# Phi first on the SP hardware queue, and tokens 1536-2559 in one store

## Chip, cores, metric

One core of one Trainium2 chip. The metric is device microseconds of one execution; lower is better. A time is the median over several runs of a kernel. The profiled execution of a kernel is one of these runs. A span is counted from its first instruction, and is some 1.8 us shorter than the time.

## The reference

Sliding-window attention on 8 batches of 8 heads (576 tokens, head size 64), and then a soft mixture of experts on its output, with 4608 tokens of width 512, 32 slots and 8 experts:

```python
x = attn(q, k, v).transpose(0, 2, 1, 3).reshape(4608, 512)   # window 32; half of the heads with dilation 4
logits = x @ phi                                             # phi: 512 x 32
d = softmax over tokens (logits);  slot_input = d.T @ x
for e in range(8):
    h = relu(slot_input[e] @ w1[e]);  slot_out[e] = h @ w2[e]   # w1: 512 x 1024, w2: 1024 x 512, f32
c = softmax over slots (logits);   out = c @ slot_out        # 4608 x 512, f32
```

## The kernel before

A list scheduler written in Python simulates all engines at build time and fixes the order of the instructions on each. Q, K, V and nearly all weights come over GpSimd's software queue, which casts f32 to bf16, in an order that is chained by hand. Two loads go over SP's hardware queue: the first half of expert 0's w1 (1 MB, uncast, converted by ScalarE) at the very start, and phi (64 KB), which waits for the first transpose on VectorE. SP also issues all output stores.

```python
    op(SP, lambda: spq.dma_start(                       # "the first w1 piece"
        af(w2off(0), [[1, 2048]]),
        w1_rows(0)[:, :2048]), .1, -200.0,              # last number: priority, low goes first
       kind="dma", nbytes=1 << 20, sem=sem("s_w1f"), writes=b_w2[0], name="w1f")
    for x in range(2):
        op(ACT, ...)                                    # f32 -> bf16 of that piece
    ...
    def load_phi(first):
        op(SP, lambda: spq.dma_start(
            f(o_phst, [[64, 2], [1, 64]]),
            moe_phi.rearrange("(hf p two) s -> p hf (two s)", hf=2, two=2)), .1, 20.0,
           kind="dma", nbytes=65536, sem=sem("s_phi"), writes=[b_phst], name="phi", after=[first])
        for g in range(2):
            op(DVE, lambda g=g: dve.tensor_copy(...), .2, -20.0,     # "the casts of phi"
               reads=[b_phst], writes=[b_phis])
    ...
    GROUPS = [(0, 4), (512, 4), (1024, 4), (1536, 8), (2560, 8), (3584, 8)]   # first token, 128-token tiles
    ...
    for G, js in [(2, (2, 3))] + [(G, range(8)) for G in range(3, 6)]:        # the last output tiles
        for j in js:
            out_tile(G, j, 0, 512, T2 + 10 + G + .1 * j)                      # matmul, eviction by ACT or DVE
            if j == js[-1] or G == 3 and j == 3:
                n = 4 if G == 3 else len(js)                                  # group 3 leaves in two stores
                store(G, 0, 512, T2 + 10 + G + .1 * j + .05, j + 1 - n, n)
```

The softmax here doesn't subtract the row's maximum and nothing guards it: scores larger than these inputs give would overflow.

Of the kernel before, what the change touches and what calls it, by code (L numbers as in the profile page):

```python
# [58 lines left out]
class Sched:  # L59
# [8 lines left out]
    def op(self, eng, fn, dur, prio, reads=(), writes=(), rmw=(), after=(), banks=(), name="",  # L68
           kind="c", nbytes=0, rate=422e3, lag=0.0, sem=None, tail=False):
        o = Op()  # L70
        o.eng, o.fn, o.dur, o.prio, o.name = eng, fn, dur, prio, name
        o.kind, o.bytes, o.rate, o.lag, o.sem, o.tail = kind, nbytes, rate, lag, sem, tail
        o.deps, o.succ = set(), []
        o.banks, o.opens, o.ord = [], [], None
        o.seq = len(self.ops)
        for a in after:
            if a is not None:
                o.deps.add(a)
        for b in reads:
            o.deps.update(b.w)  # L80
            b.r.append(o)
        for b in writes:
            if b.r:
                b.prev = b.w + b.r
                b.w, b.r = [], []
            o.deps.update(b.prev)
            b.w.append(o)
        for b in rmw:
            o.deps.update(b.prev)
            o.deps.update(b.w)  # L90
            o.deps.update(b.r)
            b.w.append(o)
        for b in list(reads) + list(writes) + list(rmw) + list(banks):
            if isinstance(b, Bank) and b not in o.banks:
                o.banks.append(b)
                if b.left == 0:
                    o.opens.append(b)
                b.left += 1
        o.deps.discard(o)
        self.ops.append(o)  # L100
        return o
# [99 lines left out]
def bass_dilated_sliding_attn__then__soft_moe_slots_kernel(  # L201
# [56 lines left out]
    o_phst, o_sid, o_rv, o_rinv, o_csp, o_rcol = 0, 128, 640, 704, 744, 760  # L258
# [3 lines left out]
    def a(off, dims, p0=0, pn=128):  # L262
        return AP(ar, p0 * NBF + off, [[NBF, pn]] + dims)
# [4 lines left out]
    def af(off, dims, p0=0, pn=128):  # L268
        return AP(ar_f.tensor, (p0 * NBF + off) // 2, [[NBF // 2, pn]] + dims)

    def f(off, dims, p0=0, pn=128):
        return AP(fs, p0 * FSW + off, [[FSW, pn]] + dims)
# [9 lines left out]
    op = sc.op  # L282
    PE, ACT, DVE, POOL, SP = "PE", "ACT", "DVE", "POOL", "SP"
    pe, act, dve, pool, spq = nc.tensor, nc.scalar, nc.vector, nc.gpsimd, nc.sync
# [7 lines left out]
    def dvet(n, psum=False):  # L292
        return ((120 if psum else 58) + n) / 960.0

    b_id, b_mp, b_md, b_oh, b_sel, b_rm, b_phst, b_phis = (Buf(n) for n in
        ("id", "mp", "md", "oh", "sel", "rm", "phst", "phis"))
# [21 lines left out]
    def w2off(e):  # L318
        return o_w2 + e * 8 * DM if e < 5 else o_stg + (e - 5) * 8 * DM


    def sem(n):
        return [nc.alloc_semaphore(n), 0]
# [13 lines left out]
    def load_batch(b):  # L337
        s = b % NSTG
        for j, x in LOADS[b > 0]:
            def fn(j=j, x=x, src=(q, k, v)[j][b, 4 * x:4 * x + 4]):  # L340
                o = o_stg + (s * 3 + j) * 2304
                if j == 0 or b == 0:
                    return pool.dma_start(a(o + 1152 * x, [[1, 1152]]),  # L343
                                          src.rearrange("h (p t) d -> (h p) (t d)", p=32))
                return pool.dma_start(AP(ar, x * NBF + o, [[2 * NBF, 64], [1, 2304]]),  # L345
                                      src.rearrange("h (u t) d -> (h u) (t d)", u=16))
            dma_in(fn, 128 * 1152 * 4, s_stg[s][j][x], (-100.0 if b < 1 else -80.0) + 2 * b,
                   f"ld{b}{'qkv'[j]}{x}", writes=[b_stg[s][j][x]] if j == 0 or b == 0 else b_stg[s][j])
# [14 lines left out]
    def w1_rows(e):  # L363
        return moe_w1[e].rearrange("(p four) f -> p (four f)", four=4)
# [28 lines left out]
    def load_w(n):  # L393
# [12 lines left out]


    op(SP, lambda: spq.dma_start(
        af(w2off(0), [[1, 2048]]),
        w1_rows(0)[:, :2048]), .1, -200.0,  # L410
       kind="dma", nbytes=1 << 20, sem=sem("s_w1f"), writes=b_w2[0], name="w1f")
# [59 lines left out]
        bb.prev, bb.w = bb.prev + bb.w, []  # L471
    first_t = []

    def load_phi(first):
        op(SP, lambda: spq.dma_start(
            f(o_phst, [[64, 2], [1, 64]]),
            moe_phi.rearrange("(hf p two) s -> p hf (two s)", hf=2, two=2)), .1, 20.0,
           kind="dma", nbytes=65536, sem=sem("s_phi"), writes=[b_phst], name="phi", after=[first])
        for g in range(2):
            op(DVE, lambda g=g: dve.tensor_copy(  # L480
                a(o_phis + 4 * g, [[128, 4], [32, 4], [1, 4]]),
                f(o_phst + 16 * g, [[32, 4], [4, 4], [1, 4]])), .2, -20.0,
               reads=[b_phst], writes=[b_phis])
# [293 lines left out]
    def row_sums(g0, n, prio):  # L777
        t0, nj = GROUPS[g0]
        w = 32 * nj * n
        bank = Bank(f"rs{g0}")  # L780

        def fn():
            last = None
            for qd in range(4):
                last = pe.matmul(pf(bank.idx, 0, [[1, w]], 32 * qd, 32), a(o_rm, [[1, 32]]),
                                 a(o_et + t0 + 32 * nj * qd, [[128 * nj, n], [1, nj], [nj, 32]]),
                                 start=True, stop=True)
            return last

        op(PE, fn, pet(4, w), prio, reads=[b_et, b_rm], writes=[bank], name=f"RS{g0}")  # L790
        op(DVE, lambda: dve.transpose(af(o_rt, [[1, w]]), pf(bank.idx, 0, [[1, w]])),
           .1 + w / 960, prio + .1, reads=[bank], writes=[b_rt], name=f"RT{g0}")
        op(DVE, lambda: dve.reciprocal(f(rcol(g0), [[1, w // 32]]), af(o_rt, [[32, w // 32]])),
           .2, prio + .2, reads=[b_rt], writes=[b_rinv], name=f"RR{g0}")

    last_ex = [None]
    for i in range(NH):
        if i % 2 == 0:
            load_batch(i // 2)
        half(i)  # L800
        if i == 0:
            load_phi(first_t[0])
        if i in RS_AT:
            for g, n in RS_AT[i]:
                row_sums(g, n, RSP * PERIOD + 16)
# [7 lines left out]
    for x, y in zip(dma_order, dma_order[1:]):  # L813
# [7 lines left out]
       writes=[b_rcol], name="cs")  # L821
# [17 lines left out]
    for x in range(2):  # L839
# [12 lines left out]
        for g in range(2):  # L852
# [5 lines left out]
            writes=[b_hsb[x], b_p[0], b_p[1]], name=f"RL{x}")  # L858
# [20 lines left out]
    def l2(es, x, col, n, cs=range(8), bufs=None):  # L879
# [22 lines left out]
       name="SOx")  # L902
# [19 lines left out]
    def ostg(G):  # L922
        return o_w1 + 8 * GROUPS[G][0]
# [25 lines left out]
    def store(G, c0, cw, prio, j0, n):  # L949
        t0, nj = GROUPS[G]  # L950
        rd = [b_og[G][j][s] for j in range(j0, j0 + n) for s in range(2)
              if c0 < 256 * (s + 1) and c0 + cw > 256 * s]
        dst = out[t0:t0 + 128 * nj, c0:c0 + cw].rearrange("(p j) f -> p j f", j=nj)[:, j0:j0 + n, :]
        src = af(ostg(G) + 2 * (512 * j0 + c0), [[512, n], [1, cw]])
        store_ops.append(op(SP, lambda: spq.dma_start(dst, src), .1, prio, kind="dma",
                            nbytes=128 * n * cw * 4, rate=347e3 if cw < 512 else 420e3,
                            sem=sem(f"s_o{G}{c0}{j0}"), reads=rd, name=f"ST{G}{c0}{j0}"))

    T2 = T1 + 40
# [9 lines left out]
    for G, js in [(2, (2, 3))] + [(G, range(8)) for G in range(3, 6)]:  # L969
        for j in js:  # L970
            out_tile(G, j, 0, 512, T2 + 10 + G + .1 * j)
            if j == js[-1] or G == 3 and j == 3:
                n = 4 if G == 3 else len(js)
                store(G, 0, 512, T2 + 10 + G + .1 * j + .05, j + 1 - n, n)

    order = sc.run([4, 5, 6, 7], [0, 1, 2, 3], last_ex[0])

# [8 lines left out]
    for o in order:  # L986
# [5 lines left out]
        for d in o.deps:  # L992
            if d.eng == o.eng == PE:
                continue
            s, val = d.ev
# [60 lines left out]
```

## Time and profile before

| | before |
|---|---|
| time, median of 3 | 177.01 us (176.88 to 177.13) |
| span of the profiled run | 175.2 us |
| bytes moved in it, as the page counts HBM traffic | 61.93 MB read, 9.44 MB written |
| last packet of the last weight slab ends | 151.23 us |
| last store packet ends | 174.41 us |

The last two are from the trace's records of single DMA packets. The main views stand in the prediction below. Two more are needed. The first is the timeline of SP and of ScalarE at the start, with start, length, what, and in brackets the idle time before it and what ended that:

```profile
0.74 0.37 SPq L408 DMA_DIRECT2D ar<-in_moe_w_dram  x1
11.85 0.38 SPq L475 DMA_DIRECT2D fs<-in_moe_phi_dram  x1
...
5.67 2.00 ACT L413 ACTIVATE ar<-ar 128x1024 bf16<-128x1024 f32 x2 [3.65 <-DMA ar<-in_moe_w_dram]
```

The first w1 piece is the first thing SP does; it has landed when ScalarE converts it at 5.67. The second view is the DMA engines' first microseconds, by stretches (the last two columns are the busy share of the 16 DMA engines and the GB/s written):

```profile
core 0: us, PE busy (x) PEld busy (x) DVE busy (x) ACT busy (x) POOL busy (x), PEclk, DMA share, GB/s
1.00:2.00 1.00, 0.00 (x0) 0.00 (x0) 0.72 (x2) 1.00 (x1) 0.77 (x2) 1.00 0.61 106
2.00:3.00 1.00, 0.00 (x0) 0.00 (x0) 0.85 (x1) 0.02 (x1) 1.00 (x3) 1.00 0.73 180
3.00:4.00 1.00, 0.00 (x0) 0.00 (x0) 0.87 (x1) 0.00 (x0) 1.00 (x3) 1.00 0.82 344
4.00:5.00 1.00, 0.00 (x0) 0.00 (x0) 1.00 (x6) 0.00 (x0) 1.00 (x3) 1.00 1.08 434
```

Nothing moves in the first 1.7 us.

### The profile page before, as it was taken

The page shows a single profiled execution, that of the slowest core. Times are in us where ns is not written, and L with a number is a line of the kernel's source. Part 1 is how long each engine was busy: PE and PEld are TensorE (multiplying, and loading weights), DVE is VectorE, ACT ScalarE, POOL GpSimd, SP SyncE. Part 2 cuts the span into 40 slices and gives each one's busy share as a digit, 9 for nine tenths or more (in the row PEclk, how much of TensorE's full clock was granted, in tenths as well). Part 3 has the DMA queues.
Part 4 walks back from the last instruction along what each step waited for, and adds up shares of the span by engine and source line. Part 5 has one row for each costly group of instructions (what it writes and reads, how often), then busy time and mean ns, then how long its engine had stood idle before and what let it go on. Part 6 is the DMA issues. An engine that isn't in the chain of part 4 may idle for free.

```text
span 175.2 us, 4785 instructions
## 1 busy us (share of the span) xinstructions
PE 127.4 (73%) x2102; PEld 86.0 (49%) x2102; DVE 120.7 (69%) x220; ACT 105.1 (60%) x165; POOL 44.5 (25%) x90
## 2 busy tenths in 40 slices
PE   0008667969998998998988997999776766898000
PEld 0005535746766866776756766776343323442000
DVE  6899497978998998998698798349430002699300
ACT  2404763797978969969868968965603001599000
POOL 7659502406234053027200014940000000000000
PEclk9999995699999999999999999999999999999655
DMA  6999999999999999999999999999999999999997
GB/s 191 228 210 217 211 214 208 219 210 213 216 211 214 217 213 207 218 211 217 213 209 216 217 213 221 215 219 211 209 223 215 210 192 189 270 343 418 449 423 299
DMA packets 14388, 41.26 MB, mean 236 GB/s; under 512 B 1696, under 2 KB 7328, under 8 KB 12064
## 3 DMA queue, kind: packets, MB, share of 16 engines
q0 software_dynamic: 10512, 30.41, 88.3%
q1 hardware_dynamic: 3856, 10.55, 15.7%
q8 instruction: 16, 0.26, 0.5%
q14 instruction: 4, 0.03, 0.0%
HBM read 61.93 MB, written 9.44 MB: 407 GB/s over the span
## 4 chain that ended last, share of the span: by engine, by line
DMA 33%; DVE 24%; PE 22%; ACT 7%; POOL 5%; issue 3%; POOLq 0%; DVEq 0%
DMA ar<-in_moe_w_dram 21%; DMA ar<-in_v_dram 12%; PE ps L529 6%; DVE ar L497 6%; DVE ar L945 6%; ACT ar L568 4%; POOL ar L381 3%; DVE ar L503 3%; PE ps L590 2%; PE ps L713 2%; PE ps L536 2%; DVE ar L634 2%; PE ps L623 2%; PE ps L546 2%; DVE ar L454 2%
## 5 line engine op out<-in xcount | busy, mean ns | idle before, releaser
L568 ACT ACTIVATE ar<-ps 128x1152 bf16<-128x1152 f32 (+1 forms) x32 | 37.9, 1186 | 21.5 <-PE ps L553 10.9
L529 PE MATMUL ps<-ar 128*128 128x320 bf16 (+1 forms) x128 | 23.2, 306 | 16.1 <-DVE ar L503 13.8
L497 DVE STREAM_TRANSPOSE ar<-ar 128x576 uint32<-128x576 uint32 x28 | 32.8, 1237 | 0.6 <-DMA ar<-in_v_dram 0.6
L634 DVE TENSOR_TENSOR ar<-ps,fs 96x768 bf16<-96x768 f32 (+1 forms) x32 | 26.3, 822 | 1.1
L596 ACT ACTIVATE ar<-ps 128x768 bf16<-128x768 bf16 x32 | 24.8, 809 | 3.6 <-PE ps L590 3.1
L529 PEld LDWEIGHTS ps<-ar 128*128 128x128 bf16 x128 | 10.8, 100 | 20.9 <-POOL ar L427 13.7
L623 PE MATMUL ps<-ar 128*128 128x65 bf16 x320 | 15.2, 195 | 3.4 <-ACT ar L568 2.1
L590 PE MATMUL ps<-ar 128*128 128x128 bf16 x192 | 15.8, 229 | 2.4 <-DVE ar L634 2.1
L503 DVE STREAM_TRANSPOSE ar<-ar 128x576 uint32<-128x576 uint32 x12 | 14.6, 1241 | 1.8 <-DMA ar<-in_q_dram 1.8
L623 PEld LDWEIGHTS ps<-ar 128*128 128x128 bf16 x320 | 12.1, 98 | 6.7 <-ACT ar L568 2.9
L345 POOL DMA_DIRECT2D ar<-in_k_dram x14 | 7.5, 541 | 30.5 <-DVE ar L497 15.6
L942 ACT ACTIVATE ar<-ps,fs 128x512 f32<-128x512 f32 (+1 forms) x23 | 11.4, 636 | 5.7 <-PE ps L934 5.7
L590 PEld LDWEIGHTS ps<-ar 128*128 128x128 bf16 x192 | 12.7, 118 | 3.7 <-DVE ar L634 2.3
L630 DVE RECIPROCAL fs<-ps 96x12 f32<-96x12 f32 (+1 forms) x32 | 6.5, 203 | 10.9 <-PE ps L623 10.6
L885 PE MATMUL ps<-ar 128*32 128x512 bf16 (+1 forms) x76 | 10.8, 347 | 4.3 <-DMA ar<-in_moe_w_dram 3.3
L945 DVE TENSOR_SCALAR ar<-ps,fs 128x512 f32<-128x512 f32 (+1 forms) x23 | 12.7, 627 | 1.0 <-PE ps L934 1.0
L934 PE MATMUL ps<-ar 128*128 128x512 bf16 (+1 forms) x46 | 10.2, 346 | 1.1 <-DVE ar L909 1.0
L343 POOL DMA_DIRECT2D ar<-in_q_dram x16 | 8.8, 549 | 6.1 <-DVE ar L509 6.1
L713 PE MATMUL ps<-ar 128*128 128x288 bf16 x64 | 9.8, 299 | 0.7 <-ACT ar L697 0.7
L693 ACT ACTIVATE ar<-ps 128x1024 bf16<-128x1024 bf16 x8 | 8.2, 1030 | 3.3 <-PE ps L680 3.3
L690 ACT ACTIVATE ar<-ps 128x576 bf16<-128x576 bf16 x16 | 9.5, 648 | 1.1 <-PE ps L674 0.8
L509 DVE STREAM_TRANSPOSE ar<-ar 128x160 uint32<-128x160 uint32 (+1 forms) x32 | 9.6, 413 | 0.0
(78 smaller groups left out, 190.2 us busy)
## 6 DMA issues: line engine op xcount, KB each, us to landing
ar<-in_moe_w_dram POOLq DMA_DIRECT2D x13, 1024.0 KB, 26.6
ar<-in_k_dram POOLq DMA_DIRECT2D x16, 288.0 KB, 14.5
ar<-in_q_dram POOLq DMA_DIRECT2D x16, 288.0 KB, 16.2
ar<-in_v_dram POOLq DMA_DIRECT2D x16, 288.0 KB, 15.2
out_dram<-ar SPq DMA_DIRECT2D x2, 2048.0 KB, 10.1
out_dram<-ar SPq DMA_DIRECT2D x10, 256.0 KB, 3.1
out_dram<-ar SPq DMA_DIRECT2D x2, 1024.0 KB, 6.1
ar<-in_moe_w_dram SPq DMA_DIRECT2D x1, 1024.0 KB, 4.9
```

The source lines that it names most:

```text
L497: return dve.transpose(au(o_kqv[kq] + 2304 * j + 36 * x, [[1, 18], [36, 16], [576, 2]]), au(src + 64 * 18 * x, [[32, 18], [1, 32]]))
L503: return dve.transpose(au(dst, [[1, 18], [18, 32]]), au(src, [[32, 18], [1, 32]]))
L529: pe.matmul(pf(h, 0, [[1, W]]), a(o_id, [[1, 128]]), a(msk, [[1, W]]), start=True, stop=False)
L568: eo = op(ACT, lambda P=P, W=W: act.activation(a(P, [[W, 4], [1, W]]), AP(ps, 0, [[4096, 128], [512, 4], [1, W]]), ACTF.Exp, scale=SCALE), ...
L590: last = pe.transpose(pb(bank.idx, bb * 256 + par * 32, [[64, 4], [1, 32]]), src, a(o_id, [[1, 128]]))
L596: op(ACT, lambda t=t, bank=bank: act.activation(a(o_vb[vs] + 3 * t * VBK, [[66, 12], [2, 32], [1, 2]]), pb(bank.idx, 0, [[64, 12], [1, 32] ...
L623: last = pe.matmul(pf(bank.idx + x, 65 * t, [[1, 65]]), w, a(VB + t * VBK + 66 * h, [[1, 65]]), start=True, stop=True)
L634: op(DVE, lambda hp=hp, bank=bank: dve.tensor_tensor(a(ox + 128 * hp, [[64, 2], [256, NT], [1, 64]], 0, rows), pf(bank.idx, 0, [[512, 2], ...
L713: last = pe.matmul(pf(bank.idx, 0, [[1, 288]]), a(o_phis + 128 * c, [[1, 128]]), a(o_xt[xt] + 576 * c + 288 * g, [[1, 288]]), start=(c == ...
L885: last = pe.matmul(pf(sobank[x].idx, 0, [[1, n]], 32 * j, 32), a(o_htz + 1024 * g + 128 * c + 32 * j, [[1, 32]]), a(w2off(e) + DM * c + co ...
L942: op(ACT, lambda: act.activation(dst, src(), ACTF.Copy, scale=sca), actt(cw, .1), prio + .1, reads=[bank, b_rinv], writes=wr, name=f"OE{G} ...
L945: op(DVE, lambda: dve.tensor_scalar(dst, src(), sca, None, op0=AluOp.mult), dvet(cw, True) + .08, prio + .1, reads=[bank, b_rinv], writes= ...
```

## The change

The intent: phi is out of the way before anything else, and the output of tokens 1536-2559 leaves in one store with longer rows. The whole diff:

```diff
+    op(SP, lambda: spq.dma_start(
+        f(o_phst, [[64, 2], [1, 64]]),
+        moe_phi.rearrange("(hf p two) s -> p hf (two s)", hf=2, two=2)), .1, -201.0,
+       kind="dma", nbytes=65536, sem=sem("s_phi"), writes=[b_phst], name="phi")
     op(SP, lambda: spq.dma_start(
         af(w2off(0), [[1, 2048]]),
         w1_rows(0)[:, :2048]), .1, -200.0,
@@
-    def load_phi(first):
-        op(SP, lambda: spq.dma_start(
-            f(o_phst, [[64, 2], [1, 64]]),
-            moe_phi.rearrange("(hf p two) s -> p hf (two s)", hf=2, two=2)), .1, 20.0,
-           kind="dma", nbytes=65536, sem=sem("s_phi"), writes=[b_phst], name="phi", after=[first])
+    def load_phi():
         for g in range(2):
             op(DVE, lambda g=g: dve.tensor_copy(
@@
-            load_phi(first_t[0])
+            load_phi()
@@
             out_tile(G, j, 0, 512, T2 + 10 + G + .1 * j)
-            if j == js[-1] or G == 3 and j == 3:
-                n = 4 if G == 3 else len(js)
-                store(G, 0, 512, T2 + 10 + G + .1 * j + .05, j + 1 - n, n)
+        store(G, 0, 512, T2 + 10 + G + .1 * js[-1] + .05, js[0], len(js))
```

## The prediction

> **What bounds the kernel now.** I read the page first, its rows by slices, and looked for a resource that is never idle:
>
> ```profile
> PE   0008667969998998998988997999776766898000
> DVE  6899497978998998998698798349430002699300
> DMA  6999999999999999999999999999999999999997
> HBM read 61.93 MB, written 9.44 MB: 407 GB/s over the span
> ```
>
> Each digit is a fortieth of 175.2 us. PE and VectorE have holes; the DMA row is 9 in all slices but the first and last. The kernel has to move 71.4 MB, and it does so at 407 GB/s on average. It is a transfer-bound kernel, and its time is: the moment the DMA engines start, plus the work queued for them, plus their bubbles, plus the last completion.
>
> Next I checked where the chain of waits enters the DMA queue:
>
> ```profile
> 79.68 20.95 DMA ar<-in_v_dram
> ...
> 115.33 36.21 DMA ar<-in_moe_w_dram
> 151.54 0.04 issue
> ...
> 152.84 8.63 DVE ar L945 x15
> 161.47 0.66 DVEq L1026
> 162.13 1.32 DVE ar L945 x2
> ```
>
> Columns are start, length, what. A V load issued at 79.7 landed 21 us later, and the last weight slab issued at 115.3 landed 36 us later: GpSimd issues far ahead, and the loads stand in a queue. A buffer that comes free a microsecond earlier or later upstream only changes how long they stand. The chain then ends in evictions up to 163.5, but the span goes on for another 11.7 us, in which nothing but DMA works. So I read the busy time by stretches:
>
> ```profile
> core 0: us, PE busy (x) PEld busy (x) DVE busy (x) ACT busy (x) POOL busy (x), PEclk, DMA share, GB/s
> 5.00:80.00 75.00, 58.43 (x1102) 42.60 (x1104) 66.37 (x112) 53.84 (x79) 28.36 (x60) 0.95 1.07 213
> 80.00:148.00 68.00, 56.70 (x947) 37.53 (x946) 37.44 (x78) 38.58 (x64) 12.18 (x21) 1.00 1.08 212
> ...
> 149.00:150.00 1.00, 0.97 (x10) 0.63 (x7) 1.00 (x4) 1.00 (x4) 0.00 (x0) 1.00 0.77 103
> ...
> 158.00:164.00 6.00, 3.29 (x12) 0.97 (x9) 5.45 (x9) 4.17 (x8) 0.00 (x0) 0.96 1.03 421
> 164.00:174.00 10.00, 0.00 (x0) 0.00 (x0) 0.00 (x0) 0.00 (x0) 0.00 (x0) 0.50 1.02 433
> ```
>
> The DMA share is at or above 1 from 5 us to 148 us and again to 174 us; the GB/s of the load stretches count bytes written as bf16, half of the f32 bytes read. In the packet records, at a quarter microsecond, the only slots under 0.97 are the start (first packet at 1.70, shares of 0.56 to 0.88 up to 2.75), 148.75 to 150.25 (the hand-over from slabs to stores), one slot at 154.0, and the end. The change touches neither of the two middle ones.
>
> **What the Trainium skill says.** All four are sections of the page "DMA: Bandwidth & Descriptors". "Issuing engines are not separate DMA queues": transfers of all issuers run on the same 16 engines and interleave. So moving phi moves work within one budget and takes none away; the shares above agree. "SWDGE vs HWDGE vs iDMA": an engine has 16 internal queues and round-robins between them. The trace agrees: phi's 256 packets of 256 B, issued at 11.85 beside a full software queue, ran from 15.55 to about 20, mostly singly among the loads' packets. "Latency and other measured facts": first byte of a hardware-queue transfer about 600 ns. The first w1 piece was issued at 0.74 for 0.37 us and its first packet began at 1.70, so 0.6 us after the issue: agrees. "Why small descriptors are slow (HBM only)": a fixed cost of about 3 cycles per packet. The records show medians of 311 ns for an 8192 B store packet and 615 for a 16384 B one: two of the former cost 7 ns more than one of the latter, so the overhead is there and tiny.
>
> **Part one, phi first.** Its work is 256 packets, 16 per engine, at a median of 18 ns: 0.29 us on each engine. Removed: these 0.29 us from 15.6 to 20. Added: the same at about 1.7. The first w1 piece is issued 0.38 us later (the old phi issue took 0.384), so its packets begin at about 2.1 and end at about 5.6 instead of 5.25. The activations that convert it (from 5.67) start 0.35 us later; their output is used only at 129.9, and ScalarE is idle until 15.53, so nothing waits.
>
> What counts is the load queue. Its first packets begin at 4.7 whatever SP does, and would then share the engines with 0.35 us more of the w1 piece. So the stream is up to 0.35 us late from 5.6 on. It gets back phi's share near 16. I looked closely there: the half w1 load finished its packets on the engines at 15.68 to 16.24, and the next load (issued only at 12.37, after GpSimd had waited for its masks) finished at 17.27 to 17.99. It needs 4 packets of 361 ns, 1.44 us, but took 1.59 on the first engine and 1.75 on the last. On the last engine 0.31 us were lost: that is phi. On the first, 0.15 us: there phi sat in a small bubble before the next load's descriptors arrived. In the new kernel the late stream covers that bubble. Sum of the part: +0.35 at the start in the worst case, -0.31 near 16, so +0.04; if phi's small packets fit into the slow start (first w1 packets took 565 to 919 ns against 309 later), down to -0.3. I take -0.0, plus or minus 0.3.
>
> The two VectorE casts of phi (180 ns each, at 20.86) move forward: their data is there, and only the dependence on the first transpose held the load back. The list scheduler will probably put them ahead of the first key transpose at 10.57. First scores, at 13.76, are then about 0.3 us later. This has slack: loads stand in the queue, and the last PE stretch before the final weights idles anyway:
>
> ```profile
> 135.58 3.61 PE L885 MATMUL ps<-ar 128*32 128x512 bf16 x40 [0.54 <-DVE ar L870]
> 141.45 3.02 PE L885 MATMUL ps<-ar 128*32 128x512 bf16 x12 [2.26 <-DMA ar<-in_moe_w_dram]
> ```
>
> PE waited 2.26 us for weights, so all the compute before may be 2 us later free of charge.
>
> **Part two, one store for tokens 1536-2559.** Two stores of 1 MB (8 KB rows, 256 packets) become one of 2 MB (16 KB rows, 128 packets). Per engine: 16 x 311 = 4.98 us become 8 x 615 = 4.92, plus one completion packet of 9 ns less: -0.06 us, and this lies on the path, as the stores run back to back to 174.2. One issue of about 0.6 us on SP goes, beside other work: SP was waiting for evictions.
>
> The price is a later start. The first half was issued at 156.96; the single store can only be issued when the eighth tile is evicted, where the second half was issued: 158.26. With 0.92 us from issue to first packet (first output store: issued 149.25, packets from 150.17) it is ready at 159.18. The store before it, 512 KB, finished on the engines at 159.33 to 159.59. So the queue just doesn't run dry: 0.15 us to spare on the earliest engine. Cost 0, at worst 0.2.
>
> Sum: 177.01 + 0.0 - 0.06 + 0 = 176.95; I allow a trifle for the thin margin and say 176.98.
>
> **The rivals.** (1) A bubble before the merged store. For it: a margin of 0.15 us against a latency known from a few stores. Against: two measured issues (0.74 and 149.25) agree on 0.92 to 0.96. If the hardware queue needed 0.5 us more, +0.35: 177.3. (2) The late first w1 piece delays all loads and nothing is given back: +0.35, 177.35. For it: the stream has no bubbles later in which to recover. Against: the 0.31 us that phi takes today on the slowest engine. (3) Phi hides wholly in the cold start and its 0.3 us near 16 go: 176.65. For it: the engines are under-used until 2.75. Against: SP issues in order, and the w1 piece moves back by a whole issue. (4) The scheduler's greedy order changes everywhere, because estimated times shift by 0.16 us (65536 B at its 422 GB/s), and compute ends later than the weights. For it: the order of all engines comes from one simulated run. Against: order of loads is fixed by explicit chaining, loads are 20 to 36 us ahead, 2.26 us are free at the end. Were it 4 us worse, about 179; I give it 2 in 100. (5) The intended gain, fewer and larger packets, being worth more than 2%: 3.5 us; the whole overhead of small rows in this store is 0.06.
>
> **Range and chances.** The central rivals span 176.65 to 177.35, and three runs of one kernel spread by 0.25. Hence 177.0, 176.6 to 177.45. Faster by 2% would need 173.5, which the bytes forbid: 1 in 100. Slower by 2% (180.6) only by a bad reshuffle: 2 in 100.
>
> **What would show each step.** The w1 piece's issue at about 1.1 and ScalarE's first conversion near 6.0 show the delay; the casts of phi near 10.6 show the move; the last slab's landing near 151.5 tells the net of part one. Fourteen stores instead of fifteen, the merged one issued near 158.3, and a DMA share of 1 between 158 and 161 show part two; a share of 0.8 at 159 would be rival 1. I am wrong if the last slab lands more than 0.5 us off 151.5, or if PE no longer waits for weights at 141.

## The result

| | before | after |
|---|---|---|
| time, median of 6 | 177.07 us (176.88 to 177.13) | 177.44 us (177.28 to 177.78) |
| ratio of the means | | 1.0024, 95% interval 1.0012 to 1.0037 |
| span of the profiled run | 175.2 us | 176.0 us |
| first packet of the first w1 piece | 1.74 us | 2.33 us |
| last packet of the last weight slab ends | 151.23 us | 151.76 us |
| last store packet ends | 174.41 us | 175.20 us |

A ratio here and below is the mean time of one kernel's fast runs over that of the other's of the same rounds, so it is not quite the ratio of the medians. The change makes the kernel slower by about 0.4 us. That is small, but the interval excludes 1, and the prediction had said nil. The median lies at the very edge of the predicted range, which ends at 177.45. (The prediction gives 1.70 for the first w1 packet before; read to the hundredth, it is 1.74.)

The profiled run of the changed kernel was the slowest of its six, 177.78, so its 0.8 us must not be read as the effect. The same views as before, for the changed kernel. First the start:

```profile
0.74 0.42 SPq L408 DMA_DIRECT2D fs<-in_moe_phi_dram  x1
1.21 0.46 SPq L412 DMA_DIRECT2D ar<-in_moe_w_dram  x1
...
7.11 1.06 ACT L417 ACTIVATE ar<-ar 128x1024 bf16<-128x1024 f32 x1 [5.09 <-DMA ar<-in_moe_w_dram]
```

```profile
1.00:2.00 1.00, 0.00 (x0) 0.00 (x0) 0.72 (x2) 1.00 (x1) 0.77 (x2) 1.00 0.13 32
2.00:3.00 1.00, 0.00 (x0) 0.00 (x0) 0.85 (x1) 0.02 (x1) 1.00 (x3) 1.00 1.10 197
3.00:4.00 1.00, 0.00 (x0) 0.00 (x0) 0.87 (x1) 0.00 (x0) 1.00 (x3) 1.00 0.74 254
4.00:5.00 1.00, 0.00 (x0) 0.00 (x0) 1.00 (x6) 0.00 (x0) 1.00 (x3) 1.00 0.99 406
```

The w1 piece is issued 0.47 us later than before, and ScalarE can convert it 1.44 us later (7.11 against 5.67). More than the issue is behind that: by the packet records its last packet ends at 6.59 instead of 5.29, as from 4.71 on it shares the engines with the first K load. Between 3 and 4 us only 254 GB/s flow instead of 344. ScalarE itself loses nothing: it was idle until its first exponential anyway. What is lost is DMA time, and this kernel has no other.

Then the long stretches and the tail:

```profile
DMA  5999999999999999999999999999999999999997
```

```profile
153.74 8.63 DVE ar L945 x15
```

```profile
5.00:80.00 75.00, 58.06 (x1109) 42.53 (x1113) 66.22 (x113) 53.92 (x79) 28.14 (x60) 1.00 1.07 214
80.00:148.00 68.00, 56.40 (x945) 37.40 (x939) 37.33 (x77) 38.53 (x63) 12.42 (x21) 1.00 1.08 212
...
150.00:151.00 1.00, 1.00 (x6) 0.46 (x3) 1.00 (x3) 1.00 (x4) 0.00 (x0) 0.50 0.76 109
151.00:152.00 1.00, 1.00 (x10) 0.77 (x10) 0.60 (x2) 0.38 (x1) 0.00 (x0) 0.50 1.11 335
...
158.00:164.00 6.00, 4.19 (x14) 1.37 (x13) 6.00 (x10) 5.07 (x9) 0.00 (x0) 1.00 1.05 426
164.00:174.00 10.00, 0.00 (x0) 0.00 (x0) 0.35 (x1) 0.00 (x0) 0.00 (x0) 0.61 1.02 434
```

The long stretches move at the same rate: nothing in the middle is slower, the stream is only later. The last evictions begin at 153.74 instead of 152.84, 0.90 later, although the last slab's packets ended only 0.53 later. The rest goes with the column before the DMA share: the clock granted to PE was 0.50 in this run from 149.1 to 152.5, as the trace's clock records say, just where the last expert's matmuls run between the last loads and the first full stores. The Trainium skill, "TensorE: Matmul & The Clock Gate", part 1, says that an idle PE falls to half clock, and that the window in which this is judged is free-running, so that the phase differs from run to run. The traces are compatible with the second half, but only one run of each kernel was kept, so they do not test it: in the profiled run of the kernel before, the half-clock stretch before the tail lay at 26.9 to 33.8, and there again with the merged store alone, in that of phi first alone (below) at 142.9 to 146.3 and 40.5 to 43.9, in that of the dummy load there was none. None of the nine other kept traces has one between 148 and 160. What it goes with can be counted in the packet records: from 148 to 156 the DMA engines were idle for 0.76 us in this run and for 0.40 in the kernel before, and most of the difference is a gap at 154.75 to 155.25 (shares of 0.25 and 0.29), where the stores waited for evictions. So some 0.4 us of this run's lateness arose in the tail, and most likely belong to this execution and not to the change; no second profile of the kernel was kept to show that.

To follow the lateness of the stream, I took all load packets from the packet records (256-byte phi packets left out), added up the f32 bytes that they had read by a given moment, a packet in flight by its share, and divided the shortfall against the kernel before by 419 GB/s, the rate of 16 engines at one 16 KB source packet per 625 ns. "Behind" below is this, in us, to about 0.01:

| kernel | first bulk packet | at 4 us | at 15 us | at 17 us | at 30 us | at 148 us |
|---|---|---|---|---|---|---|
| after | 2.33 | 0.55 | 0.62 | 0.37 | 0.28 | 0.26 |
| phi first alone | 2.31 | 0.68 | 0.74 | 0.50 | 0.40 | 0.37 |
| phi second | 1.74 | 0.04 | 0.27 | 0.03 | -0.07 | -0.06 |
| phi on ScalarE's queue | 1.74 | 0.05 | 0.26 | 0.01 | -0.08 | -0.05 |
| dummy load first | 2.23 | 0.57 | 0.64 | 0.50 | 0.64 | 0.60 |
| phi twice | 2.62 | 1.12 | 1.43 | 1.18 | 1.09 | 1.00 |
| merged store alone | 1.76 | -0.03 | 0.05 | 0.06 | 0.04 | 0.04 |

The first row is the loss and the repayment of the changed kernel: 0.6 us behind from the start, 0.34 given back between 15 and 30, and the rest kept. The other rows are the experiments.

### The profile page after: what moved, and what is told of

Its sections match the earlier page's. It is cut to its first block, busy times and chain, and to the rows that moved or that the text cites. A ratio compares the mean times of both kernels' runs of the same rounds, so it can differ in the third digit from the quotient of the medians.

```text
span 176.0 us, 4782 instructions
## 1 busy us (share of the span) xinstructions
PE 127.3 (72%) x2101; PEld 86.4 (49%) x2102; DVE 120.8 (69%) x220; ACT 105.3 (60%) x165; POOL 44.5 (25%) x90
## 4 chain that ended last, share of the span: by engine, by line
DMA 44%; DVE 25%; PE 13%; ACT 4%; POOL 4%; issue 3%; DVEq 0%
DMA ar<-in_v_dram 24%; DMA ar<-in_moe_w_dram 20%; DVE ar L497 8%; DVE ar L945 6%; PE ps L529 3%; DVE ar L503 3%; PE ps L590 2%; ACT ar L568 2%; DVE ar L458 2%; POOL ar L381 2%; DVE ar L634 2%; PE ps L934 1%; POOL ar L345 1%; DVE ar L463 1%; PE ps L885 1%
## 5 line engine op out<-in xcount | busy, mean ns | idle before, releaser
L497 DVE STREAM_TRANSPOSE ar<-ar 128x576 uint32<-128x576 uint32 x28 | 33.3, 1236 | 1.1 <-DMA ar<-in_v_dram 1.1
L529 PEld LDWEIGHTS ps<-ar 128*128 128x128 bf16 x128 | 10.9, 101 | 20.8 <-POOL ar L431 13.9
L590 PE MATMUL ps<-ar 128*128 128x128 bf16 x192 | 16.3, 234 | 2.5 <-DVE ar L634 2.2
L503 DVE STREAM_TRANSPOSE ar<-ar 128x576 uint32<-128x576 uint32 x12 | 14.6, 1242 | 1.8 <-DMA ar<-in_q_dram 1.8
L623 PEld LDWEIGHTS ps<-ar 128*128 128x128 bf16 x320 | 12.2, 98 | 7.1 <-ACT ar L568 2.9
L590 PEld LDWEIGHTS ps<-ar 128*128 128x128 bf16 x192 | 13.1, 119 | 4.0 <-DVE ar L634 2.6
L934 PE MATMUL ps<-ar 128*128 128x512 bf16 (+1 forms) x45 | 10.9, 373 | 1.3 <-DVE ar L909 1.1
L713 PE MATMUL ps<-ar 128*128 128x288 bf16 x64 | 9.2, 287 | 0.9 <-ACT ar L697 0.9
L374 POOL DMA_DIRECT2D ar<-in_moe_w_dram x7 | 3.8, 556 | 23.4 <-PE ps L553 20.9
```

The costliest lines, as they stand in the source:

```text
L497: return dve.transpose(au(o_kqv[kq] + 2304 * j + 36 * x, [[1, 18], [36, 16], [576, 2]]), au(src + 64 * 18 * x, [[32, 18], [1, 32]]))
L503: return dve.transpose(au(dst, [[1, 18], [18, 32]]), au(src, [[32, 18], [1, 32]]))
L529: pe.matmul(pf(h, 0, [[1, W]]), a(o_id, [[1, 128]]), a(msk, [[1, W]]), start=True, stop=False)
L590: last = pe.transpose(pb(bank.idx, bb * 256 + par * 32, [[64, 4], [1, 32]]), src, a(o_id, [[1, 128]]))
L623: last = pe.matmul(pf(bank.idx + x, 65 * t, [[1, 65]]), w, a(VB + t * VBK + 66 * h, [[1, 65]]), start=True, stop=True)
L934: op(PE, lambda: pe.matmul(pf(bank.idx, 0, [[1, cw]]), a(o_et + t0 + j, [[n, 128]]), a(o_so + c0, [[1, cw]]), start=True, stop=True), pet( ...
```

## The experiments

The theory after this reading: the first DMA slot on SP is worth its length, because the first w1 piece is the first bulk work the DMA engines get; a slot spent on phi delays all bulk transfers, and only phi's own bytes come back later. Rivals: the merged store costs the time (a bubble before it); the casts of phi, moved ahead on VectorE, cost it; or phi's small packets themselves are what slows the start.

All timed runs had 5 rounds; each kernel's ratio is to the kernel before in the same rounds. All computed correct results. The order of instructions on PE, ScalarE, VectorE and GpSimd is that of the changed kernel in all variants with phi moved (but for the DMA issue in ScalarE's own stream), and that of the kernel before in the others, so that the scheduler's reshuffling is not in play.

### Phi first alone

```diff
 # the changed kernel, but with the stores of before
-        store(G, 0, 512, T2 + 10 + G + .1 * js[-1] + .05, js[0], len(js))
+            if j == js[-1] or G == 3 and j == 3:
+                n = 4 if G == 3 else len(js)
+                store(G, 0, 512, T2 + 10 + G + .1 * j + .05, j + 1 - n, n)
```

> Phi first, stores as before; engine orders equal to the changed kernel's. Theory (late first w1 piece): the whole rise is here: +0.4 to +0.5 us, ratio 1.002 to 1.003; w1 packets begin near 2.2 us, last slab lands 0.3 to 0.5 us later than before. Rival 1 (the merged store costs it, by a bubble before it or by the later issue): ratio 1.000 here. Rival 2 (VectorE's casts moved ahead of the second transpose): also +0.4 here, but then also where phi comes second.

Measured: 177.35 us against 177.04, ratio 1.0019 (1.0006 to 1.0031). First w1 packet at 2.31. Last slab at 151.58, 0.35 later. The rise is here; the first rival is in trouble, the second not yet.

### Merged store alone

```diff
 # the kernel before
-            if j == js[-1] or G == 3 and j == 3:
-                n = 4 if G == 3 else len(js)
-                store(G, 0, 512, T2 + 10 + G + .1 * j + .05, j + 1 - n, n)
+        store(G, 0, 512, T2 + 10 + G + .1 * js[-1] + .05, js[0], len(js))
```

> Merged store alone; all other orders as before. Theory: -0.06 us, ratio 0.9995 to 1.000, no gap between the store before it and the merged one. Rival 1 (the store costs it): +0.4 us, ratio 1.002.

Measured: 176.91 us against 177.04, ratio 0.9991 (0.9978 to 1.0003). The point is lower than the 0.9995 to 1.000 expected, but the interval holds both that and 1. The stretches around the hand-over to the merged store, for this kernel:

```profile
158.00:159.00 1.00, 1.00 (x5) 0.41 (x4) 1.00 (x2) 1.00 (x3) 0.00 (x0) 1.00 1.04 400
159.00:160.00 1.00, 0.99 (x4) 0.38 (x4) 1.00 (x3) 1.00 (x3) 0.00 (x0) 1.00 1.30 524
160.00:161.00 1.00, 1.00 (x4) 0.24 (x3) 1.00 (x2) 1.00 (x3) 0.00 (x0) 1.00 1.13 475
```

The DMA share stays over 1: no bubble, although the store was issued only at 158.53. (A stretch counts a packet where it starts, hence shares well over 1; counted by overlap, no quarter of a microsecond from 154.75 to 174.25 is under 0.97.) The rival of the store falls.

### Phi second

```diff
 # phi first alone, with the two SP loads swapped
     op(SP, lambda: spq.dma_start(
         af(w2off(0), [[1, 2048]]),
         w1_rows(0)[:, :2048]), .1, -200.0,
        kind="dma", nbytes=1 << 20, sem=sem("s_w1f"), writes=b_w2[0], name="w1f")
     op(SP, lambda: spq.dma_start(
         f(o_phst, [[64, 2], [1, 64]]),
-        ...), .1, -201.0,
+        ...), .1, -199.0,
```

> Phi at the start on SP but behind the first w1 piece; order of PE, ACT, VectorE and GpSimd equal to the one with phi first. Theory: w1 packets begin at 1.70 again, phi's 0.3 us come right after, and the wait near 16 us is gone: within 0.1 us of before, ratio 0.9993 to 1.0006. Rival 2 (the moved casts): +0.4 us, ratio 1.002, as they sit in the same place here.

Measured: 176.94 us against 177.04, ratio 0.9992 (0.998 to 1.0005). The first w1 packet is at 1.74 again. The casts sit where they do in the kernel with phi first; this is VectorE's timeline with phi second, and the same line with phi first alone, below it:

```profile
12.38 0.28 DVE L480 CAST ar<-fs 128x64 bf16<-128x64 f32 x2
```

```profile
12.37 0.28 DVE L480 CAST ar<-fs 128x64 bf16<-128x64 f32 x2
```

Same casts, same place, no loss: the rival of the casts falls. And phi is as early as it needs to be; only the order of two neighbouring issues on SP differs from phi first, and it is worth 0.0019 + 0.0008, or nearly 0.5 us. In the table above, phi second is 0.27 behind at 15, nearly all of it from when phi's bytes are moved (4.85 to 5.79), and gets 0.34 back between 15 and 30: phi moved early costs its own 0.29 us of engine time early and saves it late.

### A dummy load first

```diff
 # the kernel before
+    op(SP, lambda: spq.dma_start(f(o_rcol + 2, [[1, 2]], 0, 16), moe_phi[0:16, 0:2]), .1, -201.0,
+       kind="dma", nbytes=128, sem=sem("s_tiny"), name="tiny")
     op(SP, lambda: spq.dma_start(
         af(w2off(0), [[1, 2048]]),
```

> Kernel before with a 128-byte dummy load (16 packets of 8 B) ahead of the first w1 piece; phi where it was. If the issue slot on SP alone makes the w1 piece late: first w1 packets near 2.1 instead of 1.70, and the stream late by 0.4 us with nothing given back near 16: +0.3 to +0.4 us, ratio 1.002. If phi's own packets are what delays it: at most +0.1, ratio 1.0005.

Measured: 177.53 us against 177.04, ratio 1.0027 (1.0013 to 1.004). SP's timeline and the DMA engines' first microseconds:

```profile
0.74 0.39 SPq L406 DMA_DIRECT2D fs<-in_moe_phi_dram  x1
1.19 0.41 SPq L408 DMA_DIRECT2D ar<-in_moe_w_dram  x1
```

```profile
1.00:2.00 1.00, 0.00 (x0) 0.00 (x0) 0.72 (x2) 1.00 (x1) 0.77 (x2) 1.00 0.01 0
2.00:3.00 1.00, 0.00 (x0) 0.00 (x0) 0.86 (x1) 0.02 (x1) 1.00 (x3) 1.00 0.88 139
3.00:4.00 1.00, 0.00 (x0) 0.00 (x0) 0.86 (x1) 0.00 (x0) 1.00 (x3) 1.00 0.84 270
```

This settles slot against bytes. A load of 128 bytes costs about 0.5 us, because the w1 piece begins at 2.23 instead of 1.74. At 15 us the stream is 0.64 behind, as far as with phi's 64 KB in the same place (0.62 and 0.74); but phi is still loaded later here, and nothing comes back. That the kernel is therefore slower than with phi first is seen in the shortfall at 148 us (0.60 against 0.37); the times, 1.0027 and 1.0019, do not tell the two apart. In the changed kernel phi's 0.28 us of packets on each engine run inside the gap of 0.53 us that its slot makes, from 1.80 to 2.33.

### Phi on ScalarE's queue

```diff
 # phi first alone
-    op(SP, lambda: spq.dma_start(
+    op(ACT, lambda: act.dma_start(
         f(o_phst, [[64, 2], [1, 64]]),
```

> Phi at the very start, but issued by ScalarE's own hardware queue, so that it costs SP no issue slot; stores as before. If the slot on SP is what costs (theory): first w1 packets at 1.70 to 1.75 us, no rise; phi's packets fall into the slow start and the wait near 16 us is gone, so 0 to -0.3 us, ratio 0.998 to 1.000. If phi's bytes at the start cost it (rival): first w1 packets may be at 1.7 but the load stream is as late as with phi first on SP, ratio 1.002.

Measured: 176.92 us against 177.03, ratio 1.0000 (0.9987 to 1.0013). No slot on SP, no loss: the theory holds. But the hope attached to it failed. ScalarE issued phi at 0.74, together with SP's w1 piece, yet phi's packets ran from 3.21 to 5.98, after w1's first ones. So phi did not fit into the slow start; most of its 0.26 us was lost between 4.5 and 6, as it is behind w1 on SP.

### Phi twice

```diff
 # phi first alone; a second copy of phi into a region that is free until much later
+    for y in b_w2[1]: y.prev = [op(SP, lambda: spq.dma_start(af(w2off(1), [[64, 2], [1, 64]]), moe_phi.rearrange(...)),
+                           .1, -202.0, kind="dma", nbytes=65536, ...)] if y is b_w2[1][0] else ...
     op(SP, lambda: spq.dma_start(
         f(o_phst, [[64, 2], [1, 64]]),
```

> Phi first on SP and a second, unused copy of it ahead of that: two slots ahead of the first w1 piece. Theory: first w1 packets near 2.8 us and another +0.4 to +0.5 us over phi first: +0.8 us over the kernel before, ratio 1.004 to 1.005. If the cost is a one-time thing of the start: ratio 1.002 again.

Measured: 178.13 us against 177.03, ratio 1.0068 (1.0055 to 1.0081): 1.1 us slower, more than the 0.8 expected. The second slot adds more to the time than the first, so the direction of the theory holds but not its size. Before anything is given back the two cost about the same: at 15 us the stream is 0.74 behind with one slot and 1.43 with two. But of the second nothing is given back. The trace shows where it goes. With the w1 piece issued third,

```profile
0.74 0.42 SPq L406 DMA_DIRECT2D ar<-in_moe_phi_dram  x1
1.21 0.46 SPq L408 DMA_DIRECT2D fs<-in_moe_phi_dram  x1
1.73 0.46 SPq L412 DMA_DIRECT2D ar<-in_moe_w_dram  x1
```

the first bulk packets are not w1's but the first K load's from the software queue, at 2.62. In the kernels before and after they began at 4.77 and 4.71, though GpSimd issues that load at 1.23 in all three. So the K load was in all likelihood ready by 2.62 all along, and had waited for the w1 piece that had the engines. And w1's packets now began only at 4.99: which queue came first took the start. The second copy of phi is also paid in full (its own 0.29 us of bytes, which no later saving repays). Against phi first alone, 0.3 us come from the later start of the bulk, and the rest from phi's bytes and the slower ramp; how much each of the two has is not separated.

### The best of the parts together

Phi second with the merged store, and phi on ScalarE's queue with the merged store:

```diff
 # phi second, or phi on ScalarE's queue
-            if j == js[-1] or G == 3 and j == 3:
-                n = 4 if G == 3 else len(js)
-                store(G, 0, 512, T2 + 10 + G + .1 * j + .05, j + 1 - n, n)
+        store(G, 0, 512, T2 + 10 + G + .1 * js[-1] + .05, js[0], len(js))
```

> Phi right behind the first w1 piece on SP, and the merged store. Theory: the two gains of the parts add: -0.1 to -0.25 us, ratio 0.9985 to 0.9995.

Measured: 176.85 us against 177.03, ratio 0.9995 (0.9982 to 1.0007).

> Phi on ScalarE's queue and the merged store. Theory: -0.1 to -0.4 us, ratio 0.9975 to 0.9995; the best of all if phi fits into the slow start.

Measured: 176.96 us against 177.03, ratio 0.9995 (0.9981 to 1.0009). Both are clear of the changed kernel's 1.0024, but neither interval excludes 1: the kernel before is not shown to be beaten.

## Why the prediction was wrong

- **What bounds the kernel: right.** Transfers, from the first packet to the last. All differences found are differences in when bulk bytes start to flow.
- **The start, the step that failed.** The prediction put the delay at "+0.35 at the start in the worst case". It measured 0.62 us behind at 15 us in the profiled changed kernel, and 0.74 with phi first alone. The dummy load, phi second and phi on ScalarE's queue show that the slot ahead of w1 is the cause. Two things were mis-sized. The slot: I took the old phi issue, 0.38 us, as the shift; the w1 piece was issued 0.47 later, its issue itself took 0.46 instead of 0.37, and its first packet came 0.59 later. The ramp: I let phi's small packets take over part of the slow start. They do not: the first 16 w1 packets took 770 ns on average in the kernel before, 778 after phi in the changed kernel, 868 with phi first alone and 840 behind the dummy load, against 309 once at rate. (The prediction gives 565 to 919 for the first ones; those 16 took 361 to 1168.)
- **"Its first packets begin at 4.7 whatever SP does": wrong.** Phi twice shows the software queue starting at 2.62. So the K load very likely waited for w1, not for GpSimd, and w1 does not use up a stretch that is free in any case: it is the first bulk work in a queue of bulk work, and what delays it delays all.
- **The repayment near 16 us: right.** Predicted -0.31; measured 0.34 between 15 and 30 in the changed kernel, the same with phi first alone and with phi second. So the sum should have been about +0.3 to +0.4 instead of +0.04.
- **The merged store: right in sign and within the noise in size.** -0.06 us predicted; 0.9991 with an interval of 0.0025 cannot tell this from 0. The feared bubble did not occur.
- **The casts of phi: nearly right.** They moved to 12.37, behind the first transpose and not ahead of it, and cost nothing, as the loads stand in a queue: PE still waited about 2 us for weights before 141.5.
- **The rival whose number came true** was the second, +0.35, and the number was luck. Its first half holds: the late w1 piece delays all loads. Its second half, that nothing is given back, does not: phi's time near 16 was given back, as the prediction said against it, but the delay to be offset was twice as long.
- **The signs it named.** The first conversion came at 7.11, not near 6.0, and the last slab's landing was reported at 152.10 in the profiled run, 0.6 off the 151.5 given, more than the 0.5 set as the mark of being wrong (with phi first alone it was 151.90, within it). The other mark did not appear: PE still waited 1.89 us for weights at 141. Fourteen stores were issued, the merged one at 159.16 instead of 158.3, and the DMA share from 158 to 161 was 1.03 to 1.25.

Sum by parts, in measured ratios: phi first +0.0019, merged store -0.0009, together +0.0010; the changed kernel has +0.0024 (1.0012 to 1.0037). The intervals overlap, and the difference of 0.2 us was not pursued; the readings of the shortfall at 148 us, 0.26 for the changed kernel and 0.37 for phi first alone, give no sign that the two parts together cost more.

## What to carry to other kernels

This is one kernel, but the habit is worth trying in others. Where the DMA engines never idle, the time until the first bulk packet is part of the span (the dummy load: 0.49 us of later start, about 0.48 us of time): issue a large load in the very first slot of the hardware queue, and small ones right behind it. Judge a small transfer there by the slot that it takes, not by its bytes: at 15 us, 128 bytes had put the stream as far behind as 64 KB (0.64 against 0.62 and 0.74). A saving elsewhere (phi's 0.3 us near 16) counts only against the full size of what was paid for it.

## What the Trainium skill lacked or had wrong

- "DMA: Bandwidth & Descriptors", "Issuing engines are not separate DMA queues", calls the sequencer time of an issue "usually small relative to the DMA itself". For the first slot of this kernel it was the whole effect: a 128-byte load ahead of the first bulk load cost 0.49 us of start and a ratio of 1.0027.
- The same page, "SWDGE vs HWDGE vs iDMA", has the engine round-robin between its queues. Phi on ScalarE's queue agrees, once it began at 3.21: from then to 4.75, 68 of its packets ran among 73 of w1's. But this sentence alone does not tell what happens between w1 and the software queue at the start: w1's packets had the engines alone from 1.74 to 4.77, although the K load had been issued at 1.23 and could very likely begin at 2.62, and with phi twice it was w1 that waited from an issue at 1.73 to 4.99. Why the two pairs of queues differ is not shown.
- No page that I read gives the slow start of the first bulk packets: 770 ns on average for the first 16 of the kernel before against 309 later, and 778 after 64 KB of small packets had gone ahead. With phi twice, where the K load went first, the first 16 w1 packets took 326 ns, and the K load's first 16 took 802 against 193 in the kernel before: the first bulk packets pay, of whichever queue.
- "TensorE: Matmul & The Clock Gate", part 1, says that the phase of the clock's window differs from run to run; a consequence worth a line there, as far as one profile can show it: a half-clock stretch at 149.1 to 152.5 stood on the path of one profiled run, which was the slowest of its six, 177.78 against a median of 177.44. A single profile of a kernel can thus show twice the effect: 0.8 us here against 0.4.
